# Attention and mixer kernel: a new written-out issue order for all engines, with the weight loads in another sequence

## The chip, the cores and the metric

The kernel runs on one core of a Trainium2 chip. The metric is the device time of one execution in microseconds. The core has five engines that run their own instruction streams in order: TensorE (PE in the profile; its weight loads are PEld), VectorE (DVE), ScalarE (ACT), GpSimd (POOL) and SyncE (SP), which here only issues transfers.

## The reference

Four batches of a gated linear recurrence over 8 heads of width 48 are computed, and their result `x` (768 tokens by 384 channels for each batch) goes through a token mixer and a channel mixer.

```python
# attention: B, H, S, D = 4, 8, 768, 48
for t in range(S):
    state = alpha[:, :, t, :, None] * state + np.einsum('bhd,bhe->bhde', k[:, :, t], v[:, :, t])
    y[:, :, t] = np.einsum('bhd,bhde->bhe', q[:, :, t], state)
# mixer: w_tok1 768x256, w_tok2 256x768, w_ch1 384x1536, w_ch2 1536x384
xt = x.transpose(0, 2, 1)
h = np.maximum(xt @ w_tok1, 0.0) @ w_tok2
u = x + h.transpose(0, 2, 1)
h2 = np.maximum(u @ w_ch1, 0.0) @ w_ch2
return u + h2
```

## The kernel before

**Tiling.** A batch is cut into three blocks of 256 tokens, so there are twelve attention blocks, numbered 0 to 11. A block loads four tiles of 128 x 768 numbers: `ld_at`, `ld_kt`, `ld_qt`, `ld_vt` (alpha, k, q, v). Its steps carry the block's number at the end:

- `P`, `ln1`, `lnP`, `r1`, `cum` (TensorE), `E`, `IE`: the running product of alpha as a sum of logarithms, and its exponentials. Blocks 0 to 2 use a wider form (`ln`, `cumw`).
- `k0a`, `q0r`, `kk`, `kl`, `qq`, `ql`: k and q scaled, on POOL or DVE.
- `trk`, `trq` (TensorE transposes) and `evk`, `evq` (their copies out of PSUM) for blocks 0 to 5. For blocks 6 to 11 the transposes are transfers that SP issues, `dk` and `dq`, and `pq` rearranges what `dq` wrote.
- `G0_`, `G1_` (products of keys and queries, TensorE), `mask0_`, `mask1_` (DVE).
- `vb`, `vs0_`, `vs1_`, `ka`, `kb`, `kc` (copies), `K` (TensorE), and the states `s`, `sa`, `sm`.
- `ia`, `ib`, `y0_`, `y1_` (TensorE), and `x0_`, `x1_`, which copy the result to the tiles `x`.

**The mixer** of batch b: `t1_b_m_c` (12 products), `ht` (two), `t2_b_i` and `u_b_i` (six each), then u transposed (`up` and `ut` for batches 0 and 1, transfers `ux` for batches 2 and 3), `c1_b_mc_half` (24 groups of three products of 384 columns) with their evictions `rt`, and `c2_b_i_q` (24 groups of three) with the sums `o` and the stores `st`. The weights come in 16 loads of the same size as a block's tiles: `ldw_wt10`, `wt11`, `wt20`, `wt21`, `wc10` to `wc15`, `wc20` to `wc25`, each followed by a cast to bf16 (`cw_`).

**What sets the order.** Nothing is scheduled when the kernel is built. The string `ORDER` lists all 946 steps by name, each with a letter for its engine (`t` PE, `s` ACT, `v` DVE, `g` POOL, `y` SP), and `Plan.run` emits them in that sequence, so it is the program order of every engine. `BUFS` lists the number of the buffer or PSUM bank that each value gets; a step that writes a buffer waits for the last reader of what was in it. Steps named `f1_` and `f3_` are products of zeros on TensorE ahead of work that is not ready.

A step that is marked `port` and runs on DVE or POOL waits, in `Emit.shared`, for the last such step of the other of these two engines:

```python
            if last and last[0] != e:
                self.tc.add_manual_dep(i.ins, last[1].ins.name,
```

All loads land in one class of 22 buffers, `in`, and all are issued by SP in the order of the list.

Of the kernel before, what the change touches and what calls it, by code (L numbers as in the profile page):

```python
# [382 lines left out]
y0_1t x0_1s vb2g K2t vs0_2s sm1_1v sa0_2t ia2t evk2v G0_2t ldw_wt10y ldw_wt11y sm0_2v vs1_2s f3_G12t G1_2t ldw_wt20y
cw_wt20s cw_wt10g t1_0_0_0t t1_0_0_1t t1_0_1_0t t1_0_0_2t t1_0_1_1t mask0_2v y0_2t ld_at4y ib2t cw_wt11g t1_0_0_3t
mask1_2v y1_2t t1_0_1_2t t1_0_1_3t x0_2v t1_0_0_4t t1_0_1_4t x1_2s t1_0_1_5t t1_0_0_5t ht_0_1v ln14s ht_0_0s t2_0_0t
u_0_0v t2_0_1t u_0_1v t2_0_2t u_0_2v ldw_wt21y cw_wt21s P4g t2_0_5t r14s t2_0_3t u_0_3v up_0_0t ld_at3y ln13s r13s
lnP4s t2_0_4t P3g up_0_1t cum4t lnP3s cum3t u_0_5v ut_0_0s IE3s E3s u_0_4v up_0_2t ldw_wc10y cw_wc10g ut_0_1v
c1_0_0_0t ldw_wc11y cw_wc11v c1_0_3_0t rt_0_3_0s ldw_wc13y c1_0_2_0t rt_0_2_0s cw_wc13g E4s rt_0_0_0s ldw_wc12y
ldw_wc14y cw_wc14s c1_0_1_0t c1_0_6_0t ut_0_2v c1_0_7_1t ld_kt3y rt_0_1_0s rt_0_6_0v rt_0_7_1v c1_0_7_0t c1_0_3_1t
rt_0_3_1s cw_wc12g c1_0_5_0t c1_0_6_1t rt_0_6_1s c1_0_0_1t c1_0_1_1t c1_0_4_1t k0a3v kk3v kl3v trk3t kb3s IE4s  # L390
c1_0_5_1t ld_qt3y q0r3v ld_vt3y rt_0_5_0v rt_0_4_1v c1_0_9_0t rt_0_1_1s vb3s vs1_3s vs0_3s ql3g rt_0_7_0v c1_0_2_1t
rt_0_5_1v qq3g trq3t ldw_wc15y cw_wc15s c1_0_8_1t rt_0_0_1v evk3v c1_0_8_0t rt_0_8_0s evq3v rt_0_2_1s rt_0_9_0s ka3g
kc3g K3t s0_3v sa1_3v ld_at5y P5g c1_0_11_0t c1_0_4_0t rt_0_4_0s c1_0_11_1t ld_qt4y q0r4g rt_0_11_0v lnP5s G0_3t ln15s
G1_3t c1_0_10_1t rt_0_11_1s ldw_wc20y c1_0_10_0t cum5t ldw_wc21y rt_0_8_1s mask0_3v mask1_3v rt_0_10_1s c1_0_9_1t
cw_wc20s ld_kt4y ldw_wc22y rt_0_10_0s y0_3t x0_3v IE5s ib3t ldw_wc23y qq4g ql4g trq4t cw_wc21g r15s y1_3t c2_0_4_0t
c2_0_5_0t cw_wc22s c2_0_2_0t c2_0_2_1t evq4v E5s kk4g c2_0_5_1t k0a4v kl4v trk4t sm1_3v evk4v cw_wc23s rt_0_9_1s
c2_0_1_0t ka4g ldw_wc24y x1_3s ld_kt5y k0a5v kk5g kb4g c2_0_1_1t G1_4t mask1_4v cw_wc24s kc4s G0_4t mask0_4v c2_0_5_2t
# [36 lines left out]
o_2_3v ux_3_1y c1_3_2_1t c1_3_1_1t c1_3_7_1t c2_2_1_2t ux_3_0y c1_3_3_0t c2_2_4_2t c1_3_1_0t c2_2_0_2t c2_2_0_3t
rt_3_7_1v c2_2_4_3t o_2_4v c2_2_1_3t c1_3_3_1t c1_3_4_0t st_1_5s st_2_4s rt_3_3_1s o_2_0v st_2_0s c1_3_9_0t st_0_3s
# [467 lines left out]
```

## Time and profile before

| | |
|---|---|
| Median of three runs | 163.16 us (162.04 to 163.50) |
| The profiled execution | 162.72 us; its span, first to last instruction, 161.0 us |
| PE busy in the span | 153.2 us (95%), 1583 products |
| DVE, ACT, POOL busy | 114.8, 101.7, 68.8 us |
| Granted TensorE clock | 1.000 |
| Transfers | 34.46 MB, mean 214 GB/s; 25.17 MB read from HBM |

The profiled execution's time has 1.7 us more than its span, which lie before the first and behind the last instruction. A line of a group reads: line of the kernel, engine, operation, what is written from what, shapes, count, busy time, mean of one in ns, and the idle time of the engine ahead of it with what ended it.

### The profile page before, as it was taken

What the parts mean: (1) busy time and instruction counts of PE and PEld (TensorE: products, weight loads), DVE (VectorE), ACT (ScalarE), POOL (GpSimd) and SP (SyncE); (2) the same over time, 40 slices, a digit from 0 to 9 for tenths busy, and PEclk for the clock granted to TensorE, in tenths of its full rate; (3) what the DMA queues carried; (4) which work ended last, traced back from release to release, by engine and by line L of the source; (5) the groups of instructions that cost most, each with busy time, mean ns of one, the idle gap of its engine ahead of it and who ended that gap; (6) DMA issues with size and microseconds to landing.
All of it is one profiled execution on the core that took longest, in us unless ns stands there. A gap on an engine that the chain in (4) does not pass through costs nothing.

```text
span 161.0 us, 4005 instructions
## 1 busy us (share of the span) xinstructions
PE 153.2 (95%) x1583; PEld 99.3 (62%) x1583; DVE 114.8 (71%) x208; ACT 101.7 (63%) x189; POOL 68.8 (43%) x83
## 2 busy tenths in 40 slices
PE   7988998999999999999999979999999999999992
PEld 4556865556675776766666646666666556666661
DVE  5189996878998898999999849878773632732061
ACT  3789878789997999699998863554832000455000
POOL 4013655217936265789489769991220000000000
PEclk9999999999999999999999999999999999999999
DMA  4999999996999999999999999997402370712035
GB/s 121 325 325 326 360 320 314 333 285 165 337 370 326 246 302 254 269 248 243 182 275 154 216 249 207 222 183 218 151 2 102 62 183 0 274 46 75 0 111 183
DMA packets 76322, 34.46 MB, mean 214 GB/s; under 512 B 68112, under 2 KB 76304, under 8 KB 76304
## 3 DMA queue, kind: packets, MB, share of 16 engines
q1 hardware_dynamic: 74144, 31.27, 76.1%
q10 hardware_dynamic: 2160, 2.95, 5.1%
q8 instruction: 12, 0.20, 0.5%
q14 instruction: 6, 0.05, 0.1%
HBM read 25.17 MB, written 4.72 MB: 186 GB/s over the span
## 4 chain that ended last, share of the span: by engine, by line
PE 87%; DVE 5%; ACT 4%; issue 1%; POOL 0%; DVEq 0%
PE ps L839 29%; PE ps L844 29%; PE ps L607 18%; PE ps L815 5%; PE ps L820 4%; PE ps L675 2%; ACT tpq L706 1%; DVE u L824 1%; DVE pkq L662 1%; DVE pkk L662 1%; PE ps L831 1%; ACT tpk L706 1%; DVE wc L707 1%; ACT IE L646 1%; ACT E L646 1%
## 5 line engine op out<-in xcount | busy, mean ns | idle before, releaser
L844 PE MATMUL ps<-wc,rt 128*128 128x384 bf16 (+2 forms) x300 | 52.7, 319 | 0.0
L839 PE MATMUL ps<-ut,wc 128*128 128x384 bf16 x288 | 50.7, 326 | 0.2
L810 ACT ACTIVATE rt<-ps 128x384 bf16<-128x384 f32 x51 | 23.2, 493 | 27.9 <-PE ps L839 25.2
L839 PEld LDWEIGHTS <-wc 128*128 128x128 bf16 x288 | 27.2, 98 | 17.5 <-DVE wc L707 0.5
L844 PEld LDWEIGHTS <-rt 128*128 128x128 bf16 x300 | 27.3, 98 | 16.3
L812 DVE TENSOR_SCALAR rt<-ps 128x384 bf16<-128x384 f32 x45 | 23.0, 552 | 12.1 <-PE ps L839 11.6
L729 DVE TENSOR_TENSOR gtm<-ps,mk 128x1024 bf16<-128x1024 f32 x24 | 28.5, 1219 | 2.6 <-PE ps L607 2.4
L848 DVE TENSOR_TENSOR in<-ps,u 128x384 f32<-128x384 f32 (+2 forms) x25 | 12.9, 538 | 13.5 <-PE ps L844 13.3
L662 POOL TENSOR_TENSOR pkq<-in,E 128x384 bf16<-128x384 f32 (+1 forms) x12 | 15.7, 1320 | 11.9 <-DVE in L658 5.7
L706 ACT CAST vb<-in 64x384 bf16<-64x384 f32 (+1 forms) x24 | 15.2, 632 | 2.2 <-DMA in<-in_v_dram 0.9
L824 DVE TENSOR_TENSOR u<-ps,x 128x384 bf16<-128x384 f32 x24 | 11.8, 550 | 1.8 <-PE ps L820 1.7
L662 POOL TENSOR_TENSOR pkk<-in,IE 128x768 bf16<-128x768 f32 (+1 forms) x7 | 11.1, 1584 | 3.4 <-DVE pkk L662 1.5
L781 POOL TENSOR_TENSOR ss<-tmp,E 128x384 bf16<-128x384 f32 x9 | 7.5, 833 | 9.7 <-DVE tmp L778 6.5
L706 ACT CAST x<-ps 128x384 bf16<-128x384 f32 x17 | 8.1, 484 | 4.1 <-PE ps L607 3.9
L815 PE MATMUL ps<-x,wt 128*128 128x384 bf16 x48 | 10.5, 326 | 0.0
L820 PE MATMUL ps<-ht,wt 128*128 128x384 bf16 x48 | 9.4, 325 | 0.6 <-ACT ht L810 0.6
L607 PE MATMUL ps<-zs 128*128 128x384 f32 (+1 forms) x22 | 8.5, 517 | 1.1 <-DVE zs L508 1.1
L662 DVE TENSOR_TENSOR pkk<-in,IE 128x384 bf16<-128x384 f32 (+1 forms) x10 | 6.1, 633 | 4.2 <-ACT IE L646 4.0
L707 POOL CAST vb<-in 64x384 bf16<-64x384 f32 (+1 forms) x10 | 5.6, 564 | 7.5 <-PE ps L607 7.0
L607 PE MATMUL ps<-tpq,tpk 48*64 48x128 bf16 (+1 forms) x288 | 8.1, 219 | 0.6 <-ACT tpk L706 0.4
L607 PE MATMUL ps<-vb,gtm 128*128 128x48 bf16 x192 | 8.6, 183 | 0.0
L592 POOL TENSOR_TENSOR in<-in 128x384 f32<-128x384 f32 x7 | 7.0, 1000 | 3.5 <-DMA in<-in_alpha_dram 3.5
(90 smaller groups left out, 208.6 us busy)
## 6 DMA issues: line engine op xcount, KB each, us to landing
in<-in_alpha_dram SPq DMA_DIRECT2D x12, 384.0 KB, 5.6
in<-in_k_dram SPq DMA_DIRECT2D x12, 384.0 KB, 4.9
in<-in_v_dram SPq DMA_DIRECT2D x12, 384.0 KB, 5.2
in<-in_q_dram SPq DMA_DIRECT2D x12, 384.0 KB, 4.9
in<-in_moe_w_ch_dram SPq DMA_DIRECT2D x12, 384.0 KB, 6.0
out_dram<-in ACTq DMA_DIRECT2D x15, 192.0 KB, 1.9
in<-in_moe_w_tok_dram SPq DMA_DIRECT2D x4, 384.0 KB, 6.3
out_dram<-in SPq DMA_DIRECT2D x8, 192.0 KB, 2.1
```

Source lines behind the costliest of these rows:

```text
L607: return self.pe.matmul(out, lhsT=lhsT, rhs=rhs, start=start, stop=stop, skip_group_check=True)
L662: self.shared(self.eng[e].tensor_tensor(self.t(dst)[:, c : c + z, :, 0:D], self.t(src)[:, :, c : c + z, :].rearrange("p h s d -> p s h d") ...
L706: return self.act.copy(d, s)
L729: self.nc.vector.tensor_tensor(self.t(gtm)[:, hf, :, :], self.pair(gp).rearrange("p a (j t) -> p (a j) t", t=128), bass.AP(tensor=m.tensor ...
L810: self.act.activation(d, s, AF.Relu)
L812: self.nc.vector.tensor_scalar_max(d, s, 0.0)
L815: self.pe.matmul(self.bank(bank)[:, 0:HD], lhsT=self.wt1[:, kc, m * 128 : m * 128 + 128], rhs=self.t(x), start=(kc == 0), stop=(kc == NS - 1))
L820: self.pe.matmul(self.bank(bank)[:, 0:HD], lhsT=self.wt2[:, kc, i * 128 : i * 128 + 128], rhs=self.t(hts[kc]), start=(kc == 0), stop=(kc = ...
L824: self.nc.vector.tensor_tensor(self.t(u)[:, i % 3], self.bank(bank)[:, 0:HD], self.t(x), ALU.add)
L839: self.pe.matmul(self.bank(bank)[:, 0:HD], lhsT=self.wc1[:, kc, mc * 128 : mc * 128 + 128], rhs=self.t(ut)[:, 3 * half : 3 * half + 3, kc, ...
L844: self.pe.matmul(self.bank(bank)[:, 0 : cz - ca], lhsT=self.t(rts[mc][0])[:, i * 128 : i * 128 + 128], rhs=self.wc2[:, mc, ca:cz], start=( ...
L848: self.nc.vector.tensor_tensor(self.row(o)[:, ca:cz], self.bank(bank)[:, 0 : cz - ca], self.t(u)[:, i % 3, ca:cz], ALU.add)
```

## The change

Only the two strings differ: `ORDER` has the same 946 steps in another sequence, and 163 of them stand on another engine (ACT has 193 steps in place of 203, DVE 185 in place of 189, POOL 82 in place of 71, SP 93 in place of 90; TensorE has the same 393, the eleven products of zeros among them). `BUFS` assigns the buffers anew. The planner that wrote the new lists counted TensorE's instruction transfers as pauses at the products that trigger them; no such thing stands in the kernel itself.

```diff
 ORDER = """
-f1_trq1t f3_cumw1t f3_K0t ld_at0y ln0s f3_trk0t ld_at1y ln1s f3_cumw0t cumw0t IE0s cumw1t E1s IE1s Et1s Et0s ld_kt0y
...
+ld_at0y f1_G11t f3_cumw0t ln0s ld_at1y ln1s f3_trq0t f3_cumw1t cumw0t IE0s Et0s ld_kt0y f1_trq0t kk0v f3_trk0t kl0v
...
 BUFS = """
-0 1 3 17 0 5 12 1 6 0 1 1 0 21 16 0 1 0 1 0 1 2 1 3 4 0 6 1 5 0 1 5 1 12 1 11 0 3 1 13 0 1 4 1 6 0 0 7 1 2 2 3 8 4 0 3
...
+21 2 0 1 1 0 4 5 2 0 6 1 7 0 1 0 12 0 0 2 0 0 2 0 0 5 7 3 3 0 1 0 2 0 4 1 18 0 6 7 0 6 1 4 6 10 1 1 0 6 5 1 1 2 2 9 2
...
```

The first place is SP's queue behind the twelve loads of batch 0: the 13th to 24th transfer, before. `moe_w_tok` are the weights `wt`, `moe_w_ch` the weights `wc` (L570 is `wc1`, in this order `wc10`, `wc11`, `wc13`, `wc12`, `wc14`).

```order
L564 DMA in_64<-in_moe_w_tok_dram 128x3x256
L564 DMA in_67<-in_moe_w_tok_dram 128x3x256
L567 DMA in_73<-in_moe_w_tok_dram 128x2x384
L548 DMA in_69<-in_alpha_dram 128x8x96
L567 DMA in_71<-in_moe_w_tok_dram 128x2x384
L548 DMA in_81<-in_alpha_dram 128x8x96
L570 DMA in_72<-in_moe_w_ch_dram 128x3x256
L570 DMA in_67<-in_moe_w_ch_dram 128x3x256
L570 DMA in_64<-in_moe_w_ch_dram 128x3x256
L570 DMA in_83<-in_moe_w_ch_dram 128x3x256
L570 DMA in_75<-in_moe_w_ch_dram 128x3x256
L548 DMA in_73<-in_k_dram 128x8x96
```

The same twelve places after the change (the L570 are `wc13`, `wc11`, `wc14`, `wc10`):

```order
L548 DMA in_65<-in_alpha_dram 128x8x96
L564 DMA in_85<-in_moe_w_tok_dram 128x3x256
L548 DMA in_74<-in_alpha_dram 128x8x96
L564 DMA in_83<-in_moe_w_tok_dram 128x3x256
L567 DMA in_72<-in_moe_w_tok_dram 128x2x384
L548 DMA in_78<-in_k_dram 128x8x96
L567 DMA in_66<-in_moe_w_tok_dram 128x2x384
L570 DMA in_73<-in_moe_w_ch_dram 128x3x256
L548 DMA in_71<-in_k_dram 128x8x96
L570 DMA in_75<-in_moe_w_ch_dram 128x3x256
L570 DMA in_69<-in_moe_w_ch_dram 128x3x256
L570 DMA in_79<-in_moe_w_ch_dram 128x3x256
```

Alpha and k of blocks 3 and 4 moved ahead of weights: `wt10` went from the 13th place to the 14th, `wt11` from the 14th to the 16th, the first `wc1` piece from the 19th to the 20th, and `wc12` from the 22nd to the 28th.

The second place is SP's queue at blocks 7 to 9, the 57th to 66th transfer, before. `tpk<-pkq` is a `dq`, `tpk<-pkk` a `dk`; the rows hold `dq7` (`tpk_106`), `dk8`, `dq8` and `dk9`.

```order
L686 DMA_TRANSPOSE tpk_105<-pkq_96 128x8x128
L548 DMA in_83<-in_q_dram 128x8x96
L686 DMA_TRANSPOSE tpk_106<-pkq_95 128x8x128
L548 DMA in_84<-in_v_dram 128x8x96
L548 DMA in_66<-in_q_dram 128x8x96
L686 DMA_TRANSPOSE tpk_105<-pkk_99 128x8x128
L686 DMA_TRANSPOSE tpk_107<-pkq_96 128x8x128
L548 DMA in_85<-in_v_dram 128x8x96
L548 DMA in_65<-in_k_dram 128x8x96
L686 DMA_TRANSPOSE tpk_106<-pkk_97 128x8x128
```

The same ten places after the change (`dq7` is `tpk_106`, then `dk8` and `dq8`, and `dk9` last):

```order
L548 DMA in_72<-in_alpha_dram 128x8x96
L548 DMA in_75<-in_q_dram 128x8x96
L686 DMA_TRANSPOSE tpk_106<-pkq_96 128x8x128
L686 DMA_TRANSPOSE tpk_107<-pkk_97 128x8x128
L686 DMA_TRANSPOSE tpk_104<-pkq_95 128x8x128
L548 DMA in_81<-in_alpha_dram 128x8x96
L548 DMA in_71<-in_alpha_dram 128x8x96
L548 DMA in_72<-in_k_dram 128x8x96
L548 DMA in_69<-in_q_dram 128x8x96
L686 DMA_TRANSPOSE tpk_104<-pkk_99 128x8x128
```

`dq7` and `dk9` keep the 59th and 66th place. The products that need them moved on TensorE: `G1_7` stands 3.5 us of TensorE's work earlier in the list than before, and `K9`, which needs `dk9` through the copy `kc9`, 4.0 us later.

The third place is DVE's queue at the start of `c1` of batch 1, before: `ut_1_1`, `q0r7`, `kk7` (`pkk_98`), and evictions `rt`.

```order
L707 COPY ut_134<-ps 128x768
L658 TENSOR_TENSOR in_74<-in_74,lf_88 128x8x48
L662 TENSOR_TENSOR pkk_98<-in_70,IE_94 128x16x48
L812 TENSOR_SCALAR rt_135<-ps 128x384
L812 TENSOR_SCALAR rt_150<-ps 128x384
```

After the change: `ut_1_0`, the sum `o_0_3`, `k0a8`, which reads the load `ld_kt8` (the 51st transfer), `kk7` (`pkk_99`), and the evictions of `c1_1_9_0`, `c1_1_10_1` and `c1_1_4_0`.

```order
L707 COPY ut_134<-ps 128x768
L848 TENSOR_TENSOR in_78<-ps,u_130 128x384
L654 TENSOR_TENSOR in_79<-in_79,in_64 128x8x48
L662 TENSOR_TENSOR pkk_99<-in_73,IE_93 128x16x48
L812 TENSOR_SCALAR rt_140<-ps 128x384
L812 TENSOR_SCALAR rt_144<-ps 128x384
L812 TENSOR_SCALAR rt_153<-ps 128x384
```

A step that needs a late load (`k0a8`) now stands on DVE ahead of the evictions that free TensorE's banks; before it stood on POOL. By `BUFS`, `c1_1_8_0` takes the bank that `rt_1_9_0` frees.

More of the change, by code (lines that the diff above doesn't have):

```diff
@@ L383 @@
[L383 to L397, printed above, removed]
@@ new lines @@
+evq3v c1_0_8_1t c1_0_8_0t rt_0_8_0s c1_0_10_1t vs0_3g kb3g K3t ldw_wc12y cw_wc12g c1_0_4_0t rt_0_4_0s rt_0_6_1v
+ld_qt4y q0r4g qq4g c1_0_4_1t rt_0_4_1s s0_3v sa1_3v rt_0_8_1v rt_0_1_0s ldw_wc21y c1_0_5_0t ld_at5y rt_0_5_0s G1_3t
+rt_0_10_1s G0_3t c1_0_10_0t rt_0_10_0s c1_0_5_1t mask0_3v c1_0_11_1t c1_0_1_1t y0_3t mask1_3v ln15s rt_0_5_1s
+ldw_wc20y ql4g trq4t ldw_wc22y P5g lnP5s cum5t rt_0_1_1v cw_wc20s ib3t sm1_3g rt_0_11_1s c1_0_11_0t E5s r15s x0_3v
+cw_wc21g c2_0_1_0t y1_3t cw_wc22g IE5s c2_0_5_0t c2_0_5_1t x1_3s evq4v G1_4t G0_4t ld_kt5y k0a5g kk5v mask1_4v
@@ new lines @@
+y0_5t x0_5v cum6t sm0_5g t1_1_1_0t t1_1_1_1t lnP7s ld_qt6y q0r6v ib5t y1_5t x1_5v t1_1_1_2t t1_1_1_3t E6s cum7t IE6s
+ld_vt6y ln17s o_0_4v qq6g P8v t1_1_1_4t t1_1_0_3t t1_1_0_4t t1_1_0_5t ht_1_0s t1_1_1_5t ht_1_1s ld_vt7y c2_0_0_3t
+o_0_0v c2_0_3_0t ln18s t2_1_1t u_1_1v kk6g ka6g t2_1_4t lnP8s r18s ld_kt7y k0a7g t2_1_0t u_1_0v t2_1_3t t2_1_5t
+t2_1_2t u_1_2v c2_0_3_1t c2_0_3_2t ld_qt7y E7s vb6s up_1_0t IE7s r17s u_1_3v q0r7g u_1_5v up_1_1t c2_0_3_3t vs0_6s
+ut_1_1s cum8t ld_qt8y u_1_4v up_1_2t ut_1_2s E8s ut_1_0v c1_1_2_0t c1_1_4_0t ld_kt8y vs1_6g o_0_3v k0a8v kk7v dk6y
@@ new lines @@
+t2_3_5t t2_3_0t u_3_0v rt_2_5_0v t2_3_3t u_3_3v c2_2_2_0t t2_3_4t u_3_5v u_3_4v c2_2_1_0t c2_2_1_1t rt_2_7_0s
+c2_2_1_2t c2_2_1_3t o_2_1v ux_3_0y c2_2_2_1t c2_2_2_2t c2_2_2_3t c2_2_0_0t c2_2_0_1t o_2_2v c1_3_2_0t c1_3_1_0t
+rt_3_1_0v c1_3_7_0t rt_3_7_0s c2_2_5_3t st_1_1s ux_3_1y c1_3_2_1t c1_3_9_1t c1_3_4_1t rt_3_4_1s st_0_3s c1_3_0_0t
+rt_3_0_0s rt_3_2_0v c1_3_8_1t rt_3_9_1v c1_3_6_1t c1_3_0_1t rt_3_0_1s c1_3_5_1t st_2_4y c2_2_0_2t c1_3_1_1t rt_3_1_1s
+c1_3_3_1t rt_3_3_1v c2_2_0_3t o_2_0v st_2_0y c1_3_9_0t rt_3_9_0s c1_3_10_1t c1_3_3_0t c1_3_10_0t rt_3_5_1v rt_3_6_1s
```

100 lines of the change are left out of this document (50 added, 50 removed), and 20 rows, old and new, of the table BUFS.

## The prediction

> **What bounds the kernel now.** I read the page first, then the granted clock, the busy times by stage, TensorE's waits and the chain of waits.
>
> ```profile
> span 161.0 us, 4005 instructions
> PE 153.2 (95%) x1583; PEld 99.3 (62%) x1583; DVE 114.8 (71%) x208; ACT 101.7 (63%) x189; POOL 68.8 (43%) x83
> core 0: us, PE busy (x) PEld busy (x) DVE busy (x) ACT busy (x) POOL busy (x), PEclk, DMA share, GB/s
> 0.00:5.66 5.66, 4.54 (x11) 2.70 (x11) 2.12 (x19) 2.28 (x3) 1.97 (x12) 1.00 0.67 180
> 5.66:30.99 25.33, 22.93 (x312) 15.66 (x311) 20.90 (x34) 21.83 (x37) 9.13 (x11) 1.00 1.10 330
> 30.99:82.00 51.01, 51.01 (x513) 33.74 (x517) 45.53 (x79) 45.66 (x89) 31.91 (x34) 1.00 1.03 270
> 82.00:97.08 15.08, 13.97 (x261) 9.43 (x250) 12.00 (x17) 12.38 (x21) 12.21 (x12) 1.00 1.19 224
> 97.08:157.53 60.45, 60.45 (x504) 37.58 (x502) 33.65 (x61) 19.59 (x41) 13.58 (x16) 1.00 0.46 122
> 157.53:161.00 3.47, 0.31 (x11) 0.19 (x7) 0.62 (x2) 0.00 (x0) 0.00 (x0) 1.00 0.50 170
> ```
>
> TensorE bounds it at full clock. It has no gap from 31 to 82 us and none from 97 to 157.5; between these it stands 1.1 us, in the opening 2.4 us beside products of zeros, and the tail behind its last product is 3.5 us. So a new order can save only in the opening, the 1.1 us, and the tail. The transfers are nearly as full: the DMA share is over 1 until 97 us.
>
> ```profile
> PE ps L607 <- POOL pkk L707: 1.1, 1, 1.1
> 136.85 9.26 PE ps L839 x57
> 26.21 1.78 PE L820 MATMUL ps<-ht,wt 128*128 128x384 bf16 x10 [0.58 <-ACT ht L810]
> 30.22 6.79 PE L839 MATMUL ps<-ut,wc 128*128 128x384 bf16 x39
> 94.25 0.34 PE L607 MATMUL ps<-vb,pkk 128*128 128x96 bf16 x4 [1.06 <-POOL pkk L707]
> ```
>
> To compare two orders I give each TensorE step a position: the work ahead of it in the list from the first `cumw` on, without the zeros, at the chain's cadences (0.1625 us for 384 columns, from 9.26 us for 57; the small attention products likewise by theirs). Both lists sum to 141.6 us. Start minus position is the lag. Before, it is 5.7 at the first `cumw`, 13.1 at the first `t2` (26.21, position 13.1), 13.6 at the first `c1` (30.22, position 16.6), 13.9 from 37 to 82 us, 15.7 at `K9` (94.25, position 78.6), and 15.9 at the end (157.5). Then 3.5 of tail give 161.0. The change wins or loses by this lag.
>
> **The change part by part.** Removed or added work: none on TensorE (same 393 steps, same eleven products of zeros). Eleven more steps on POOL, ten fewer on ACT and four fewer on DVE cost nothing as such, since these engines have idle time; their order counts.
>
> *The wait that can go.* The 1.1 us is `K9` waiting for `kc9` on POOL, and this for the transfer `dk9`:
>
> ```profile
> 86.86 2.66 SPq L686 DMA_TRANSPOSE tpk<-pkk  x1
> DMA to landing us min/median/max: 6.7/6.7/6.7
> 93.69 0.50 POOL L707 COPY pkk<-pkk 64x384 bf16<-64x384 bf16 x1 [1.81 <-ACT x L706]
> ```
>
> Issued at 86.86, `dk9` landed 6.7 later at 93.57, `kc9` ran 93.69 to 94.19, `K9` began at 94.25. After the change `dk9` keeps the 66th place of SP's queue, while `K9` moves from position 78.6 to 82.6. At the lag of 13.9 that is 96.5, over 2 us behind `kc9`. Term: −1.1 us.
>
> *The opening.* Two POOL steps that wait for transfers show when the 14th and the 16th landed: just ahead of 21.20 and of 23.48, so 1.1 to 1.2 us for each transfer.
>
> ```profile
> 21.20 0.83 POOL L707 CAST wt<-in 128x768 bf16<-128x768 f32 x1 [0.17 <-DMA in<-in_moe_w_tok_dram]
> 23.48 1.00 POOL L592 TENSOR_TENSOR in<-in 128x384 f32<-128x384 f32 x1 [1.45 <-DMA in<-in_alpha_dram]
> 24.07 0.55 DVE L707 CAST x<-ps 128x384 bf16<-128x384 f32 x1
> 25.67 0.49 ACT L810 ACTIVATE ht<-ps 128x384 bf16<-128x384 f32 x1
> 26.73 2.88 DVE L824 TENSOR_TENSOR u<-ps,x 128x384 bf16<-128x384 f32 x6 [0.67 <-PE ps L820]
> 29.53 0.55 DVE L707 COPY ut<-ps 128x768 bf16<-128x768 bf16 x1
> 30.99 6.02 PE ps L839 x36
> ```
>
> After the change the 16th is `wt11`: landed 23.45, cast on POOL 0.83, 24.3; `P4` on DVE must wait for that cast as a `port` step, and takes 0.55, as other DVE steps of 384 columns do: 24.9; `x1_2` behind it 0.55: 25.5; three `t1` products and the last one's pass, 0.8: 26.3; `ht_0_0` 0.49: 26.85; so `t2` begins at 26.9, 0.7 later than before. The six `u` follow at 27.4 and take 2.9, `ut_0_1` 0.55, so `c1` begins at 30.85 against 30.22. But `trk3` (0.45) now stands ahead of it, position 17.1 against 16.6, and before the second `c1` group waited for a cast until 30.99. The lag behind the first groups is 13.8 against 13.9. Term: 0, bounds ±0.6, half a transfer's time, because one place of SP's queue decides `P4`.
>
> *The load stream.* From the 27th transfer on, what counts is how far the stream is ahead. The longest stand of SP in it (the 28th and 29th transfer, and the 28th's time to landing):
>
> ```profile
> 32.56 0.57 SPq L548 DMA_DIRECT2D in<-in_alpha_dram  x1
> 35.70 0.37 SPq L548 DMA_DIRECT2D in<-in_q_dram  x1
> DMA to landing us min/median/max: 7.5/7.5/7.5
> ```
>
> That is 2.6 us from 33.13 to 35.70, for a buffer (`qt4` waits until `kl3` has read it). In the new `BUFS`, places 27 to 39 take buffers whose readers finish earlier (`cw_wt20` about 25.8, `cw_wt11` 24.3, `k0a4` about 31), so the stream may run up to 2.6 us ahead; the next wait is `at7` for `cw_wc24`, near 52.
>
> *The new waits.* The new order asks for some transfers earlier. Priced at the same place's landing before:
>
> ```profile
> 76.76 2.37 SPq L686 DMA_TRANSPOSE tpk<-pkq  x1
> DMA to landing us min/median/max: 4.8/4.8/4.8
> 81.58 1.36 ACT L706 COPY tpq<-tpk 128x1024 bf16<-128x1024 bf16 x1
> L548 SPq DMA_DIRECT2D in<-in_v_dram x1: 1359/1359/1359, 64.4 to 64.4; - x1
> DMA to landing us min/median/max: 5.4/5.4/5.4
> L548 SPq DMA_DIRECT2D in<-in_q_dram x1: 580/580/580, 90.9 to 90.9; - x1
> DMA to landing us min/median/max: 4.9/4.9/4.9
> ```
>
> `c1_0_4_0` (position 26.1, due 40.0) needs `wc12`, now 28th: landed 32.56 + 7.5 = 40.05, cast 0.83, 40.9: wait 0.9. `c1_1_8_0` (57.0, due 70.9) needs the bank that `rt_1_9_0` frees, behind `k0a8`, which needs the 51st: landed 64.4 + 5.4 = 69.8, then 0.55, 0.96 for the wide `kk7` (two passes of 0.48) and 0.55: 71.85, wait 0.95. `G1_7` (67.8, due 81.7) needs `pq7` behind `dq7`, still 59th: landed 76.76 + 4.8 = 81.55, copied by 82.95: wait 1.25. `K9` itself (82.6, due 96.5) needs `vt9`, now 68th: landed 90.9 + 4.9 = 95.8, one cast of 0.83 as on POOL and two of half the size at 0.5: 97.65, wait 1.15. They do not add, because a wait at one moves TensorE back for the next: together 0 if the stream is 1.3 us ahead, at most 1.3 if it is not. I take 0.4, since half of the 2.6 us would cover them.
>
> *The tail*: the last product, its sum and the store of 64 columns are last in both lists: 0.
>
> Sum: 0 − 1.1 + 0.4 = −0.7 us on the profiled 162.72 (1.7 outside its span): 162.0. The median of the runs shown is 163.16, 0.4 above; the forecast on it is **162.5 us**.
>
> **The instruction transfers.**
>
> ```profile
> q8 instruction: 12, 0.20, 0.5%
> L548 SPq DMA_DIRECT2D in<-in_k_dram x1: 1149/1149/1149, 11.6 to 11.6; - x1
> DMA to landing us min/median/max: 4.8/4.8/4.8
> L548 SPq DMA_DIRECT2D in<-in_v_dram x1: 1148/1148/1148, 12.8 to 12.8; - x1
> DMA to landing us min/median/max: 6.1/6.1/6.1
> ```
>
> Twelve transfers of 16 KB feed TensorE. I see no stop of TensorE in the stages above, but loads can be slowed: issued 1.2 us after `kt2`, `vt2` landed 2.5 us after it. The lists differ little in when TensorE passes each 256th instruction, so I take the same delays for both. The Trainium skill ("Runtime: NRT & Kernel Launch", Instruction fetch mechanics) says each engine's instructions come in 16 KiB blocks of 256 by a DMA queue of its own, with the cost mostly hidden. The row's sizes agree and so does TensorE without gaps; that loads lose a microsecond there, the page does not say.
>
> **Rivals.**
>
> *The stream runs ahead and everything fits.* The new waits are 0 and the opening gains its 0.6: −1.1 − 0.6 = −1.7, to 161.4; a shorter second half of the opening could add some tenths. For it: SP's wait at 33.1 vanishes. Against: DVE and ACT are busy 21 and 22 of the opening's 25 us.
>
> *DVE stands behind a late load (slower).* In the new list three DVE steps wait for a load ahead of evictions that TensorE needs: `q0r6` ahead of `x1_5`, `k0a8` and `kk7` ahead of `rt_1_9_0`, `q0r9` ahead of `ht_2_0`. With `kt8` landing at L, `c1_1_8_0` begins no earlier than L + 2.05, so the lag is L + 2.05 − 57.0, over the 15.9 of before once L passes 70.85: 1.05 us later than the 69.8 above. One new SP wait like the 2.6 us ones makes L 72.4 and the lag 17.4; two more DVE steps, each 0.55, in front of the next banks make 18.0: +2.1, so 165.3. For it: SP's `dk8` must wait for `G0_6` to free its tile. Against: kt8's buffer is long free. The Trainium skill ("TensorE: Matmul & The Clock Gate", Architectural detail) calls DVE and ACT strict FIFOs; `K9`'s wait behind SP's order is the same thing on SP, and nothing here shows DVE overtaking.
>
> *The pauses are wrong and move nothing.* If the modelled pauses hit nothing real, the new list returns the 1.1 us at the new waits, all 1.25 of the largest: −1.1 + 1.25, 163.3. By the skill's "mostly hidden" this would be the outcome.
>
> **How the numbers follow.** About 1% (1.6 us) can be told from no change. The forecast (−1.6 to +0.3) 0.38; pauses move nothing 0.08; ahead and all fits 0.28; DVE behind a load 0.26. So faster 0.28, same 0.46, slower 0.26. The forecast's own range is 161.5 to 163.5. The 8-in-10 range reaches to 160.6 (the first rival with 0.8 more from the opening) and to 165.5 (the second's price).
>
> **What would show it.** `c1` beginning at 30.9 ± 0.6; SP without a wait near 35; `K9` without a wait over 0.3; `c1_0_4_0`, `c1_1_8_0` and `G1_7` with waits below 0.5 each; the tail 3.5. I am wrong if the last product ends after 158.5 (new waits larger), or if `c1` begins after 31.7 (then the opening's chain is another), or if TensorE stands over 1 us behind a DVE eviction.

## The result and the profile after

The changed kernel takes 163.30 us in the median of 20 executions (162.24 to 165.29), the kernel before, beside it, 162.37 (161.49 to 163.50). The ratio is 1.0049, 95% interval 1.0029 to 1.0069: slower by half a per cent, where −0.4% on the median shown was forecast. The ratios leave out executions that took over 1.5% longer than the fastest of their kernel (two of the 20 here). The profiled execution took 162.29 us with a span of 160.6, nearly its shortest; the one profiled before took 162.72 with 161.0, somewhat above its median. The two profiles alone would have said faster. So the question is what a usual execution of each looks like, and further profiles were taken of both.

The busy times of the changed kernel in the stages that the prediction used (same columns):

```profile
span 160.6 us, 4016 instructions
core 0: us, PE busy (x) PEld busy (x) DVE busy (x) ACT busy (x) POOL busy (x), PEclk, DMA share, GB/s
0.00:5.32 5.32, 4.20 (x9) 2.42 (x9) 2.12 (x19) 2.13 (x2) 1.99 (x12) 1.00 0.65 170
5.32:30.99 25.67, 22.66 (x312) 15.49 (x310) 18.86 (x29) 21.04 (x35) 14.95 (x18) 1.00 1.10 322
30.99:82.00 51.01, 50.92 (x516) 33.24 (x514) 44.24 (x74) 43.15 (x84) 36.08 (x41) 1.00 1.06 277
82.00:97.08 15.08, 15.08 (x215) 10.12 (x214) 12.84 (x20) 11.88 (x24) 10.44 (x12) 1.00 1.13 229
97.08:157.10 60.02, 60.02 (x535) 37.52 (x532) 35.68 (x63) 18.94 (x40) 12.71 (x13) 1.00 0.47 118
157.10:160.60 3.50, 0.37 (x13) 0.24 (x9) 0.62 (x2) 0.00 (x0) 0.00 (x0) 1.00 0.49 169
```

Between 82 and 97 us TensorE now has no gap (15.08 of 15.08), and the tail is 3.50 us as before. Before 31 us it stands 3.0 us, 0.6 more than before. Its waits in the same execution:

```profile
PE ps L607 <- DVE ss L772: 1.5, 2, 0.9
PE ps L607 <- DVE zs L508: 1.1, 1, 1.1
PE ps L820 <- ACT ht L810: 0.6, 1, 0.6
PE ps L607 <- DVE gtm L729: 0.4, 1, 0.4
PE ps L607 <- ACT tpq L706: 0.2, 1, 0.2
PE ps L675 <- POOL pkk L662: 0.2, 1, 0.2
```

`K9`'s wait for `pkk` by L707 is gone. The longest waits are for `ss` by L772, the states `s` and `sm` of the first blocks. All waits of the list lie ahead of 36 us.

### The lag, stage by stage, in all traces

The prediction's lag (start of a TensorE step minus the work ahead of it in its own list) shows where each execution lost time. This table is worked out from the traces, each with its own list; the first column is the lag at the first `cumw`, and each further one is what the lag grows by between two steps.

| trace | first `cumw` | to `K1` | `K1` to `K2` | `K2` to `t2` | `t2` to `c1_0_9_0` | to the last product | sum |
|---|---|---|---|---|---|---|---|
| before, first profile | 5.66 | 4.86 | 0.56 | 2.03 | 0.78 | 2.14 | 16.04 |
| before_again | 6.42 | 4.79 | 0.57 | 2.04 | 0.78 | 1.39 | 15.98 |
| before_third | 6.13 | 4.79 | 0.56 | 2.04 | 0.78 | 0.95 | 15.25 |
| changed, first profile | 5.32 | 5.08 | 1.66 | 2.10 | 0.75 | 0.77 | 15.67 |
| after_again | 5.55 | 5.50 | 2.20 | 2.57 | 0.51 | 0.78 | 17.11 |
| after_timed | 5.55 | 5.81 | 1.66 | 2.09 | 0.51 | 0.77 | 16.39 |

Three things stand here. Between `K1` (about 17 us) and `K2` (20.6 us) the new order loses 1.1 us more than the old one in every trace (1.6 in after_again, where TensorE's clock fell; see the end). Behind `c1_0_9_0` the old order loses 2.14 us in the first profile only, 1.39 and 0.95 in the others, the new one always 0.77 or 0.78. The start varies by 0.8 us in the kernel before.

The first two columns must be read together, as the lag at `K1`. In every trace the products of zeros of 384 columns at first begin 0.64 us apart, and from some moment on 0.32 us apart. That moment is 4.5, 6.0 and 5.4 us in the three traces of before, and 5.1, 6.4 and 7.2 us in those of the changed kernel. The old list has one product of zeros more ahead of the first `cumw`, so there a late moment shows in the first column, and in the new list in the second. At a like moment the new order has about 0.4 us less lag at `K1`, not more: 10.40 us (moment 5.1) against 10.92 (5.4, before_third), and 11.05 (6.4, after_again) against 11.40 (6.4, v1_again below, whose opening is the old one). What it loses in the opening, it loses between `K1` and `K2`.

### The profile page after: what moved, and what is told of

The parts are those of the page before. It is cut to its first block, busy times and chain, and to the rows that moved or that the text cites. A ratio compares the mean times of both kernels' runs of the same rounds, so it can differ in the third digit from the quotient of the medians.

```text
span 160.6 us, 4016 instructions
## 1 busy us (share of the span) xinstructions
PE 153.2 (95%) x1583; PEld 99.0 (62%) x1583; DVE 114.4 (71%) x204; ACT 97.1 (60%) x182; POOL 76.2 (47%) x94
## 4 chain that ended last, share of the span: by engine, by line
PE 86%; DMA 4%; ACT 4%; SPq 2%; issue 1%; POOL 1%; DVE 1%; DVEq 0%
PE ps L839 30%; PE ps L844 29%; PE ps L607 16%; PE ps L820 4%; DMA in<-in_moe_w_tok_dram 4%; PE ps L815 4%; PE ps L675 2%; PE ps L831 1%; ACT E L646 1%; ACT IE L646 1%; SPq L548 1%; ACT tpq L706 1%; POOL pkq L662 1%; ACT tpk L706 1%; ACT wt L706 1%
## 5 line engine op out<-in xcount | busy, mean ns | idle before, releaser
L839 PE MATMUL ps<-ut,wc 128*128 128x384 bf16 x288 | 51.6, 326 | 0.1
L810 ACT ACTIVATE rt<-ps 128x384 bf16<-128x384 f32 x54 | 24.9, 492 | 34.2 <-PE ps L839 33.9
L812 DVE TENSOR_SCALAR rt<-ps 128x384 bf16<-128x384 f32 x42 | 21.8, 552 | 14.7 <-PE ps L839 14.7
L662 POOL TENSOR_TENSOR pkq<-in,E 128x384 bf16<-128x384 f32 (+1 forms) x10 | 13.2, 1323 | 10.9 <-DVE pkq L662 5.5
L662 POOL TENSOR_TENSOR pkk<-in,IE 128x384 bf16<-128x384 f32 (+1 forms) x12 | 15.1, 1270 | 2.3 <-ACT lf L595 0.8
L706 ACT CAST vb<-in 64x384 bf16<-64x384 f32 (+1 forms) x20 | 12.2, 609 | 0.9 <-DMA in<-in_v_dram 0.6
L707 POOL CAST vb<-in 64x384 bf16<-64x384 f32 (+1 forms) x14 | 9.0, 640 | 7.9 <-DVE pkq L662 7.3
L607 PEld LDWEIGHTS <-tpk 48*64 48x64 bf16 (+1 forms) x288 | 5.7, 102 | 4.6 <-issue 3.5
L607 PEld LDWEIGHTS <-gtm 128*128 128x128 bf16 x192 | 7.5, 96 | 1.4
L778 DVE TENSOR_TENSOR tmp<-ps,ss 128x384 f32<-128x384 f32 x12 | 6.7, 555 | 2.3 <-PE ps L607 1.4
```

Of the source, the lines that this page charges most:

```text
L607: return self.pe.matmul(out, lhsT=lhsT, rhs=rhs, start=start, stop=stop, skip_group_check=True)
L662: self.shared(self.eng[e].tensor_tensor(self.t(dst)[:, c : c + z, :, 0:D], self.t(src)[:, :, c : c + z, :].rearrange("p h s d -> p s h d") ...
L706: return self.act.copy(d, s)
L810: self.act.activation(d, s, AF.Relu)
L812: self.nc.vector.tensor_scalar_max(d, s, 0.0)
L839: self.pe.matmul(self.bank(bank)[:, 0:HD], lhsT=self.wc1[:, kc, mc * 128 : mc * 128 + 128], rhs=self.t(ut)[:, 3 * half : 3 * half + 3, kc, ...
```

## The experiments

Ratios are to the kernel before, run beside each on the same chip, with 95% intervals. Theory O: the loss lies in the opening, ahead of the first `c1` product; rival R: behind it. The diffs show only the part of a list around the edit.

**1. after_again, before_again, before_third, after_timed: the two kernels as they are.**

> The changed kernel as it is, for a second profile of it. Its first profile (span 160.6 us) is one of its two fastest of 20 executions, the median is 1.0 us longer. Theory O (the opening): the microsecond is lost before the first c1 product of batch 0, by transfers that land later there; the lag behind c1_0_9_0, 14.9 in the first profile, is 15 to 16 here, and grows by no more than 1.0 from there to the end. Rival R (the rest): the opening is as in the first profile within 0.3, and a wait of 0.5 us or more stands somewhere behind 36 us that the first profile did not have (kt8, dq7, vt9 or a transpose landing late).

> The kernel before as it is, for a second profile. In the run of b_K9_late the kernel before took 161.85 us in the median, and moving K9 brought nothing (1.0013), though its profile shows the wait gone. Theory V (the first profile of before caught a late transfer): here dk9 lands less than 5.5 us after its issue (6.7 in the first), K9 waits less than 0.3 us, and the span is near 160.0. Rival: K9 waits again about 1.1 us, and the span is near 161.

> The changed kernel, timed on the same chip as the two mixtures beside it, with the granted clock of each execution. Theory O (the opening's 1.0 us, and no gain at K9 in the typical execution): 1.003 to 1.008. About one execution in five has a mean clock of 0.989, as in after_again, where TensorE ran at half clock from 20.2 to 23.5 us, behind a pause of 1.03 us; these are the longer ones by 0.5 us or more. If the clock alone made the difference, the executions at clock 1.000 would be as short as those of before.

> The kernel before, a third profile. Theory V (the K9 wait of the first profile was one late landing): dk9 lands 4.0 to 5.0 us after its issue and K9 waits less than 0.3 us; with an early start (first cumw at 5.7 or less) the span is 159.7 to 160.3, with a late one 160.6 to 161.2. Rival: K9 waits 0.7 us or more, span 161.

after_timed measured 1.0046 (1.0023 to 1.0068), so the half per cent repeats. after_again took 163.75 us (span 162.0): lag 16.3 at `c1_0_9_0`, a little over what theory O allowed, and 0.8 more to the end with no new wait, as O has it. before_again took 162.63 us (span 160.9), before_third 161.89 (span 160.2). First `dk9` and then the first product of `K9` in before_again:

```profile
86.69 2.34 SPq L686 DMA_TRANSPOSE tpk<-pkk  x1
DMA to landing us min/median/max: 4.6/4.6/4.6
93.92 0.33 PE L607 MATMUL ps<-vb,pkk 128*128 128x96 bf16 x4
```

The same in before_third:

```profile
86.70 2.09 SPq L686 DMA_TRANSPOSE tpk<-pkk  x1
DMA to landing us min/median/max: 4.3/4.3/4.3
93.43 0.33 PE L607 MATMUL ps<-vb,pkk 128*128 128x96 bf16 x4
```

Issued within 0.2 us of the first profile's 86.86, `dk9` landed 4.6 and 4.3 us later, not 6.7. TensorE went on to `K9` without a stop in both. The 1.1 us that the prediction wanted to save belonged to one late transfer in one execution: theory V. The spans fitted it less well (160.9 where 160.0 was expected, 160.2 where a late start was to give 160.6 or more), since both starts were late and the small waits behind `K9` differ too.

The falls of the clock are not the half per cent either: after_timed's executions at a mean clock of 1.000 have spans of 161.0 to 161.6 with a median of 161.2, those of before at 1.000 beside them a median of 160.2 (all 22 of before: 160.7).

**2. b_K9_late: `K9` alone.**

```diff
-K9t x0_7s t1_2_0_2t t1_2_0_3t ... t1_2_0_5t s0_9v sa1_9v t1_2_1_3t
+x0_7s t1_2_0_2t t1_2_0_3t ... t1_2_0_5t t1_2_1_3t K9t s0_9v sa1_9v
```

> The kernel before with one thing of the change: K9 (and the two DVE steps s0_9 and sa1_9 that read it) stands behind eight of the t1 products of batch 2 in place of ahead of them. The prediction's term for this wait: -1.1 us, ratio 0.993, with K9's wait below 0.3 us. Rival: the microsecond comes back at the next wait (ib9, ht_2, G0_9 or a later transpose), ratio 0.998 to 1.002.

1.0013 (0.9987 to 1.0040). In its profile (span 160.0) the wait is gone and nothing came in its place: the lag grows by 1.13 behind `c1_0_9_0`, inside the 0.95 to 1.39 of the two usual traces of before. The ratio is the rival's, but not for its reason: the time did not come back, it was not there to be saved.

**3. h_before_open and h_after_open: halves of the two lists.** The steps up to the first `c1` group from one list, all others from the other, with buffers assigned anew where both claimed one.

> The 167 steps up to the first c1 group in the order and on the engines of the kernel before, then all other steps in the order of the changed one. Theory O: the opening is what the change lost, the rest is what it won (no wait at K9), so this kernel is faster than the one before by 0.8 to 1.5 us (ratio 0.991 to 0.995). Rival R (the rest of the new order loses in most executions what it wins at K9): ratio 1.000 to 1.006, as the changed kernel.

> The opposite mixture: the 177 steps up to the first c1 group as in the changed kernel, then all others in the order of the kernel before. Theory O: it has the opening's loss and the wait at K9 as well, unless the later K9 hides it: between the changed kernel's 1.005 and 1.012. Rival R: the opening costs nothing in most executions, ratio 0.997 to 1.003.

1.0178 (1.0127 to 1.0229) and 1.0308 (1.0263 to 1.0354): neither theory's numbers. The seam is at fault: the two lists load kt3 and the first `wc1` pieces in another sequence, so at the seam TensorE stood 2.2 us for `trk3` in one and 2.8 us for `c1_0_0_0` in the other. They say nothing on where the loss lies, but something on the clock (below).

**4. v1_pre_t1_before and v2_post_t1_before: a seam where both streams agree.** In v1 (timed a second time as v1_again) the steps of blocks 0 to 2 ahead of the first `t1` product are those of the kernel before, with the alpha loads of blocks 3 and 4 and the weights sequenced as in the changed one; in v2 the opposite. By the names of the loads alone, v1 against the changed kernel:

```diff
 v1: the first 12 loads
-at0 at1 kt0 qt0 vt0 qt1 at2 kt1 vt1 qt2 kt2 vt2
+at0 at1 kt0 vt0 at2 qt0 qt1 kt1 qt2 vt1 kt2 vt2
 at3 wt10 at4 wt11 wt20 kt3 wt21 wc13 kt4 ...
```

> The steps of blocks 0 to 2 ahead of the first t1 product in the order and on the engines of the kernel before; the weight loads, alpha and k of blocks 3 and 4 from the 13th transfer on, and everything from t1 on, as in the changed kernel. Theory A (the lag is lost by blocks 1 and 2, at sa1_1 and trk2, by 19.3 us, ahead of any weight): the lag at t2_0_0 is 13.0 to 13.5 in place of 14.15, and the time is that of before or less, ratio 0.996 to 1.001. Rival W (the weights' sequence): the lag at the first c1 is 14.5 or more all the same, ratio 1.003 to 1.008.

> The opposite: everything ahead of the first t1 product, with alpha of blocks 3 and 4 ahead of weights, as in the changed kernel, and from t1 on the order of before, the weights' included (only the cast of wt20 stands on POOL, behind the fifth t1 product). Theory A: the lag at t2_0_0 is 14 or more, ratio 1.003 to 1.009. Rival W: the lag at the first c1 is back at 13.9, ratio 0.998 to 1.002.

> The kernel v1_pre_t1_before again: old order ahead of the first t1 product, new order behind it. Theory: the new rest is shorter by the small waits that the old one has behind 82 us, 0.2 to 0.6 us: ratio 0.996 to 0.999. Rival: no difference, 0.999 to 1.001.

| trace | first `cumw` | to `K1` | `K1` to `K2` | `K2` to `t2` | `t2` to `c1_0_9_0` | to the last product | ratio |
|---|---|---|---|---|---|---|---|
| v1_pre_t1_before | 5.66 | 4.85 | 0.57 | 2.07 | 0.65 | 0.86 | 0.9974 (0.9949 to 1.0000) |
| v1_again | 6.61 | 4.79 | 0.57 | 2.08 | 0.52 | 0.85 | 0.9989 (0.9968 to 1.0011) |
| v2_post_t1_before | 5.55 | 5.59 | 1.66 | 2.98 | 0.78 | 1.09 | 1.0105 (1.0078 to 1.0132) |

Theory A: with the old steps ahead of `t1` the loss is gone, although the weights are still in the new sequence (v1: lag 13.15 at the first `t2`); with the new steps it is there (v2: 15.8). v2's ratio lies above theory A's range; its excess over the changed kernel is a wait of 0.7 us for an `x` at the seam. W, the weights' sequence, is out. That the rest of the new order is shorter than the old one's stays open: the second run's interval holds 1.

**5. v3_no_zeros_trq1: two products of zeros less.**

```diff
-G1_0t f1_trq1t qq1v sm1_0v ld_at2y f3_trq1t mask1_0v trq1t
+G1_0t qq1v sm1_0v ld_at2y mask1_0v trq1t
```

> The changed kernel without two of its zero products, f1_trq1 and f3_trq1 (0.98 us of TensorE ahead of trq1). Theory Z (in the changed order these zeros stand in front of work that is ready: qq1 and ql1 end at 12.11 and 11.52, trq1 starts at 13.23): trq1, cumw2 and G0_0 come 0.8 to 1.0 us sooner against G1_0, DVE's idle 1.4 us ahead of mask0_0 falls below 0.6, and the lag at t2_0_0 falls by 0.4 to 1.0; ratio to the kernel before 0.997 to 1.002. Rival P (POOL is the bound: kl2 and kk2 one after the other, behind kt2's landing at 17.8): kk2 ends within 0.3 of 20.4 less the start's jitter, K2's lag falls by less than 0.3, ratio 1.003 to 1.006.

1.0001 (0.9971 to 1.0032), while v4 and v5, run beside it with these zeros in place, have 1.0039 and 1.0043: one edit makes the changed kernel level with the one before. TensorE in the changed kernel, from `G1_0` on (the zeros, `trq1`, `cumw2`, `G0_0`), and DVE's `mask0_0` that waits for `G0_0`:

```profile
11.92 0.40 PE L607 MATMUL ps<-tpq,tpk 48*128 48x128 bf16 x8 [0.19 <-ACT tpq L706]
12.25 1.14 PE L607 MATMUL ps<-zs 128*128 128x128 f32 x4
13.23 0.61 PE L675 MATMUL ps<-idn,pkq 128*128 128x128 bf16 x8
13.67 0.66 PE L607 MATMUL ps<-la,u 128*128 128x400 bf16 x3
14.61 0.40 PE L607 MATMUL ps<-tpq,tpk 48*128 48x128 bf16 x8
15.12 1.22 DVE L729 TENSOR_TENSOR gtm<-ps,mk 128x1024 bf16<-128x1024 f32 x1 [1.40 <-PE ps L607]
```

Without them:

```profile
12.60 0.40 PE L607 MATMUL ps<-tpq,tpk 48*128 48x128 bf16 x8 [0.18 <-ACT tpq L706]
12.93 0.62 PE L675 MATMUL ps<-idn,pkq 128*128 128x128 bf16 x8
14.32 0.44 PE L607 MATMUL ps<-tpq,tpk 48*128 48x128 bf16 x8
14.87 1.23 DVE L729 TENSOR_TENSOR gtm<-ps,mk 128x1024 bf16<-128x1024 f32 x1 [0.54 <-PE ps L607]
```

From `G1_0` to `G0_0` it is 1.72 us in place of 2.69, and DVE idles 0.54 us in place of 1.40. To `K1` the lag grows by 4.60 (5.08 to 5.81 with the zeros). `K1` to `K2` stays at 1.66: what the edit wins makes up for that loss and does not take it away.

**6. v6_fewer_zeros: six zero products less** (also the two ahead of `cumw1` and the two ahead of `K0`).

> The changed kernel without six of its eleven zero products: f1_trq0 and f3_trk0 ahead of cumw1, f1_K0 and f3_K0 ahead of K0, f1_trq1 and f3_trq1 ahead of trq1. Theory Z (in the changed order zeros stand in front of work whose operands are there: cumw1 ready at 6.4 and begun at 7.1 to 8.1, K0 ready at 10.1 and begun at 10.3 to 11.2): the lag at K0 is 7.6 or less whatever the start, the lag at t2_0_0 13.6 to 14.1, and the ratio to the kernel before 0.995 to 1.000, below the 1.000 of the kernel without the two at trq1. Rival K (the zeros hold TensorE's clock up): products at half clock between 6 and 14 us or behind a pause there, mean clock below 0.995 in most executions, ratio 1.003 or more.

1.0011 (0.9984 to 1.0037), mean clock 0.998 or more in all 12: rival K is out. But the four further zeros cost nothing, and the lag at `K0` is 8.4, not 7.6 or less: 4.53 to `K1` against v3's 4.60, since TensorE then stands for DVE ahead of `trk0` (1.10 us) and for POOL ahead of `K0` (0.49 us) all the same. Theory Z holds for one of three places.

**7. v4_sm0_first: one step of DVE.**

```diff
-mask1_1v ia1t G0_1t ld_kt2y ql2g kl2g vs0_0s y0_0t vs1_1s sm0_1v sa1_1t
+sm0_1v mask1_1v ia1t G0_1t ld_kt2y ql2g kl2g vs0_0s y0_0t vs1_1s sa1_1t
```

> The changed kernel with one DVE step moved: sm0_1 ahead of mask1_1 in place of behind it, so that sa1_1 need not wait for the mask (1.03 us). Theory D (DVE's order is the loss): the lag at K2 falls by 0.7 or more, ratio 0.998 to 1.001. Rival P (POOL's kl2 and kk2, that trk2 needs, stand right behind): sa1_1 comes 0.9 sooner, trk2 waits in its place until kk2 ends, the lag at K2 falls by less than 0.3, ratio 1.003 to 1.005. Since the pause is cut in two, no execution should have the mean clock 0.989, which the changed kernel has in 8 of 33.

1.0039 (1.0009 to 1.0069): rival P. In the changed kernel `sa1_1` waits for DVE; the second half of `trk2` and POOL's `kl2` and `kk2` follow:

```profile
19.29 0.32 PE L607 MATMUL ps<-ss,idn 128*128 128x384 bf16 x1 [0.87 <-DVE ss L772]
20.44 0.40 PE L675 MATMUL ps<-idn,pkk 128*128 128x128 bf16 x4 [0.16 <-POOL pkk L662]
18.44 1.95 POOL L662 TENSOR_TENSOR pkk<-in,IE 128x384 bf16<-128x384 f32 x2
```

With `sm0_1` first:

```profile
18.28 0.32 PE L607 MATMUL ps<-ss,idn 128*128 128x384 bf16 x1
20.48 0.40 PE L675 MATMUL ps<-idn,pkk 128*128 128x128 bf16 x4 [0.56 <-POOL pkk L662]
18.45 1.97 POOL L662 TENSOR_TENSOR pkk<-in,IE 128x384 bf16<-128x384 f32 x2
```

`sa1_1` comes 1.0 us sooner, `trk2`'s second half at the same time: `K1` to `K2` 1.68. The wait that the profile names first is not the one that binds.

**8. v8_kk2_dve: one of POOL's three steps to DVE**, on top of v3 (`kk2v` right behind `qq2v`, `sm0_1v` ahead of `mask1_1v`, `mask0_1v` behind `sm0_2v`).

> The kernel without the two zeros at trq1, and on top of it kk2 on DVE right behind qq2, ahead of POOL's ql2 and kl2 (POOL then has two of these 1.0 us steps in a row in place of three); sm0_1 ahead of mask1_1, and mask0_1 behind sm0_2, so that the mask stands in front of nothing. Theory P (POOL's row of three sets K2): from K1 to K2 the lag grows by 1.0 to 1.35 us, in place of 1.66, and by no more than 2.4 from K2 to the first t2 (2.2): 0.2 to 0.5 us less in all, ratio 0.997 to 0.999 where the kernel without the zeros had 1.000. Rival D (DVE is as full as POOL here): K2 comes sooner, but the 0.55 us more on DVE comes back between K2 and t2, which grows to 2.6 or more; ratio 1.000 to 1.003.

1.0077 (1.0031 to 1.0123): neither. Part of it is the clock: two of the eight executions in the ratio had a mean clock of 0.979, and the other six, at 0.998 or more, have a median of 163.1 us against 162.4 beside them. DVE and POOL in the profile, whose clock is 1.000:

```profile
17.58 0.56 DVE L662 TENSOR_TENSOR pkk<-in,IE 128x384 bf16<-128x384 f32 x1 [0.83 <-DMA in<-in_k_dram]
18.28 1.00 POOL L662 TENSOR_TENSOR pkq<-in,E 128x384 bf16<-128x384 f32 x1 [2.70 <-DVE pkk L662]
```

`kk2` had to wait for the load kt2, and POOL's `ql2` for `kk2` by the `port` rule, so it came 0.8 us later than in the changed kernel (17.48); `K1` to `K2` grew by 2.50. kt2 is late in the changed kernel too; its row, vt2's, and the time of the two to landing:

```profile
L548 SPq DMA_DIRECT2D in<-in_k_dram x1: 1150/1150/1150, 11.6 to 11.6; - x1
L548 SPq DMA_DIRECT2D in<-in_v_dram x1: 1149/1149/1149, 12.8 to 12.8; - x1
DMA to landing us min/median/max: 6.1/6.2/6.2
```

6.2 us (17.79) where it took 4.8 before (16.37): the delay that fell on vt2 alone now falls on kt2 as well. In the changed kernel, though, nothing waits for kt2. POOL's `ql2` begins behind DVE's `qq2`, and `kl2` (18.44 above) when `ql2` ends, 0.65 us behind kt2's landing:

```profile
17.48 1.00 POOL L662 TENSOR_TENSOR pkq<-in,E 128x384 bf16<-128x384 f32 x1 [1.80 <-DVE pkq L662]
```

v6 bears this out: there kt2 landed at 16.37, and `K1` to `K2` is 1.79 all the same, with the same row of three on POOL. So the row holds `K2` in the changed kernel, and kt2's landing only where the row is shortened as in v8. No run shortened the row with kt2 early, so that the row is the whole of the 1.1 us is not shown.

**9. v5_zeros_in_pause: the clock.**

```diff
-vs1_1s sm0_1v sa1_1t
+vs1_1s sm0_1v f1_trq2t sa1_1t
```

> The changed kernel with one more zero product of 128 columns (f1_trq2, 0.43 us) in the pause of 1.03 us ahead of sa1_1; it can begin when mask1_1 frees its bank, 0.5 us into the pause. Theory C (a pause of about 1 us, at an unlucky moment, lets the clock fall to half for 3.3 us): no execution of 12 with mean clock 0.989 where one in four had it; the executions at clock 1.000 as long as the changed kernel's, 161.0 to 161.6 us of span; ratio 1.003 to 1.005. Rival: the clock falls for another reason (the start of the kernel, the half-filled cumw products): 0.989 comes again in 2 to 4 of 12.

1.0043 (1.0013 to 1.0073). No execution of 12 had a mean clock below 0.997, and none of v4's, where 7 of 33 of the changed kernel had 0.989 (the expectations say 8, a miscount): theory C, so far. But v3 and v6 keep the pause of 1.03 us (0.87 in the profile's rows, where `y0_0` is taken to end later), and only 1 of their 24 had a low clock (0.979). The pause alone does not decide; what else does is open.

**10. v7_wt21_first: a stop of v1 taken away.** The load of wt21 one place ahead, `trk3` and `evk3` behind the first `c1` group.

> v1 with two more edits: the load of wt21 one place ahead, before kt3, and trk3 with its copy evk3 behind the first c1 group in place of ahead of up_0_2. Theory: t2_0_3's wait for the cast of wt21 (0.27 us) goes, c1 begins 0.2 to 0.4 us sooner, and all of it stays to the end, since nothing behind waits: ratio 0.994 to 0.998, below v1's beside it by 0.001 to 0.002. Rival: trk3 or k0a3, whose load kt3 now lands 1.1 us later, wait in its place: the same ratio as v1's or up to 0.003 more.

1.0028 (1.0004 to 1.0051), the rival's side, though TensorE does not stand at `trk3`. The wait for wt21's cast is gone, but `trk3` had filled the time until DVE's last `u`; without it `up_0_2` waits:

```profile
30.34 0.51 PE L831 MATMUL ps<-idn,u 128*128 128x128 bf16 x6 [0.41 <-DVE u L824]
```

Then `c1_0_7_1` waits 0.3 us more for `ut_0_2`, which now stands behind the later `evk3` on DVE. `t2` to `c1_0_9_0` grows by 1.40 in place of 0.52 to 0.65. No version measured here is surely faster than the kernel before; v1 comes nearest.

## Why the prediction was wrong

**What bounds it, and the lag: right.** TensorE at full clock sets the end, and a lag once gained stays: in every trace of the changed kernel, the lag behind 36 us grows by no more than 0.8 us.

**`K9`, −1.1 us: the step that failed first.** The wait was read rightly and its removal too. What failed is that one execution's late transfer was taken for the kernel's. 6.7 us from issue to landing is 4.6 and 4.3 in the two further profiles. The first profile alone could not show this: its transposes took 3.1 to 6.7 us to land, and the 6.2 of `dk8` comes back in the others (6.0 and 6.2). The usual worth of the edit is 0.0 (b_K9_late, 1.0013, where 0.993 was the term).

**The opening, 0 ± 0.6: the second that failed.** The first `c1` group began at 31.76 in the profile, not 30.85, over the 31.7 named as the sign that the opening's chain is another, and a usual execution is later still (32.48 in after_timed). The chain followed began at the 16th transfer, wt11, which landed at 24.00 (forecast 23.45). The term measures +1.0 us between the two first profiles (lag 14.91 against 13.89 at `c1_0_9_0`), and +0.6 against before_third, whose start is most like. But the loss lies ahead of that chain: 1.1 us between `K1` and `K2`, partly made up by the 0.4 us that the new order gains up to `K1`. It would gain more there if two zero products did not stand in front of `trq1`. "Same eleven products of zeros" counted them and priced them at nothing; in the new list `ql1` moved to POOL and is done at 11.52, so the zeros there cover no wait: 0.97 us from `G1_0` to `G0_0`, and by v3 about 0.4% of the time. Likewise "eleven more steps on POOL cost nothing as such" was averaged over the whole span; between 17.5 and 20.4 us POOL holds `ql2`, `kl2` and `kk2` in a row, `trk2` waits for the last of them, and `K2` stands behind `trk2`.

**The new waits, +0.4: mechanism right, size 0.** SP's stand near 35 us did not vanish but moved: SP now stands 2.4 us, from 31.2 to 33.6, for the buffer that `kl4` reads on POOL, ahead of wc12.

```profile
SPq L570 <- POOL pkk L662: 2.4, 1, 2.4
```

The stream is ahead by 0.8 to 1.3 us, not 2.6: wc12 landed at 38.79 (40.05 assumed), kt8 at 69.02 (69.8), dq7 at 80.29 (81.55), vt9 at 94.91 (95.8). No wait over 0.2 us came at `c1_0_4_0`, `c1_1_8_0`, `G1_7` or `K9`, so the rival of DVE behind a late load did not happen either. The opening's loss is not what hid them: v1, with 1.1 us less lag at `c1_0_9_0` (13.8 against 14.91), adds 0.86 us behind it, the changed kernel 0.77. **The tail, 0: right** (3.50).

**The sum.** By the table, at a like start: −0.4 up to `K1`, +1.1 between `K1` and `K2`, 0 to −0.3 from `t2` to `c1_0_9_0`, and −0.2 to −0.6 behind it in the usual traces, in all about −0.1 to +0.5 us. The medians differ by 0.8 us (0.0049 of 162.4). Three traces of each kernel do not show where the rest comes from: how the starts are spread, and the clock that fell in 7 of 33 executions, may both have a part.

The median of 163.30 lies within the forecast's own range of 161.5 to 163.5, but by luck: the range stood on a median of three runs, 163.16, and 20 runs of the kernel before have 162.37. The rival "pauses wrong, move nothing" named 163.3, the median that came, but by a wait at `G1_7` that is not there; its number is chance. Whether the modelled pauses bought anything was not tried apart. That the longer landings of vt2 and kt2 come from the instruction transfers, as the prediction took it, was not tested.

## What to carry to other kernels

A wait that hangs on a transfer is worth what its usual landing gives: take a second profile before pricing its removal, since a difference of half a per cent is smaller than the spread between two executions. When executions start differently, compare lags only at a like start. Price fillers anew whenever the work behind them moves: products of zeros are free only while what follows is late. After an edit that removes the first-named wait, look for the next operand of the following step, as with `sm0_1` and `kk2`.

## What was not expected of the hardware

**TensorE's clock fell behind a short pause.** after_again, from `y0_0`'s end on, by stretches:

```profile
18.89:20.20 1.31, 0.44 (x10) 0.27 (x7) 1.31 (x3) 1.20 (x2) 1.31 (x3) 0.95 0.47 162
20.20:23.50 3.30, 3.30 (x34) 2.62 (x32) 2.23 (x4) 2.23 (x3) 2.29 (x3) 0.50 0.99 287
23.50:25.00 1.50, 1.50 (x21) 0.73 (x16) 1.49 (x3) 0.97 (x3) 1.34 (x3) 1.00 1.06 325
```

Behind a pause of 1.03 us the granted clock was 0.50 for 3.3 us, and the lag grew by 0.5 us more from `K1` to `K2` and by 0.5 more to `t2` than in after_timed. The kernel before, whose three profiles have no pause over 0.75 us between 9 and 36 us, never had a mean clock below 0.996 in 125 executions. The seam of h_before_open shows the same behind 2.2 us:

```profile
30.30:32.50 2.20, 0.19 (x4) 0.01 (x1) 0.09 (x1) 2.20 (x6) 1.94 (x3) 1.00 1.07 330
32.50:35.90 3.40, 3.34 (x16) 2.04 (x17) 1.15 (x2) 1.09 (x2) 2.92 (x4) 0.51 1.05 322
```

With pauses of 2.2 and 2.8 us at the two seams, 11 of 12 executions had a mean clock of 0.987 to 0.990; v8, with 1.2 us ahead of `sa1_1` and 1.0 us right behind it (1.01 and 0.81 in the profile's rows), had 0.969 to 0.979 in 6 of 12. The Trainium skill ("TensorE: Matmul & The Clock Gate", Part 1) has a clock of half speed, set by activity in free-running windows of about 3.4 us, and warns of idle gaps over that length. The half and the 3.3 us agree; here a third of that length was enough in some executions.

**The start is not the same twice.** The first products of `cumw0` in the changed kernel's first profile, and in after_timed:

```profile
5.32 0.66 PE L607 MATMUL ps<-la,u 128*128 128x400 bf16 x3
```

```profile
5.55 1.18 PE L607 MATMUL ps<-la,u 128*128 128x400 bf16 x3
```

Three products took 0.66 or 1.18 us, while the clock column reads 1.00 in both. The same three products of `cumw1` in after_timed, 2.5 us later:

```profile
8.09 0.66 PE L607 MATMUL ps<-la,u 128*128 128x400 bf16 x3
```

So TensorE ran at half its later pace until some moment in the first microseconds, and the column does not show it. The products' starts (0.64 us apart, then 0.32) put the moment between 4.0 us (b_K9_late) and 7.2 us (after_timed). By `K1` the second execution is 0.95 us later.
